# One transfer instead of two for the first tokens, and the first products over all four token tiles in turn

## The chip, the cores and the metric

The kernel runs on one core of a Trainium2 chip. Time is device time in microseconds (us) from launch to end; lower is better. The engines are PE (TensorE, matrix products; PEld are its loads of the stationary operand), DVE (VectorE), ACT (ScalarE), POOL (GpSimd) and SP, which here only issues transfers (DMAs).

## The reference

The input has 2048 tokens of 448 features. Two branches are computed from it and mixed by a gate per token. Branch A is attention with 16 heads of 28 features, in which every token sees itself and seven earlier ones at steps of two. Branch B is a dense layer to 1792 features, a squared ReLU, and a dense layer back.

```
qkv = x @ wqkv                      # 448 -> 3*448
a   = softmax(q . k[s-2w] * scale over w=0..7) @ v  @ wo
h   = relu(x @ w1 + b1)**2          # 448 -> 1792
b   = h @ w2 + b2
g   = sigmoid((x * gate_w).sum(-1))
out = g * a + (1 - g) * b
```

## The kernel before

All matrix operands are split into a high part, rounded to a shorter format, and a low part, the rest. A product of two numbers is then three products on PE: high x high, high x low, low x high. In the code the names end in `h` and `l` (`x.h`, `x.l`, `wqh`, `wql`).

The 448 features that are summed over lie in row tiles: three of 128 rows (k = 0, 1, 2) and a last one of 64. The tokens come in four chunks of 512, each of four token tiles of 128. One accumulator in PSUM holds the result of one token tile and one of q, k, v.

The kernel first computes q, k and v for all chunks, writes them to DRAM, and reads them back in the order that attention wants. Attention runs on POOL (products) and DVE (sums), beside the dense branch on PE. The order of instructions on each engine is the order of the code: a planner with an assumed PE clock (`advance`, `at`, `when`) decides at build time where the work of the other engines is put between the products.

The change lies at the very start. Before data is there, PE runs `WARM` products of zeros into a scratch accumulator (line 632). Meanwhile SP issues, for each row tile k, a transfer of the q weights (line 639) and one of the tokens of the first chunk (line 644); for k = 0 the tokens come in two transfers of 256 columns, token tiles 0 and 1 and then 2 and 3. Lines 654 to 665 split what arrives: ACT makes the high part of the weights (655) and of the tokens in two halves of columns (662), except for the first half of k = 0, which DVE makes (660); DVE makes the low parts (663 for the weights, 665 for the tokens, in halves).

`qkv_first` (line 257) then adds up q for the four token tiles of the first chunk. For each k it takes token tiles 0 and 1 through their three products, two by two, and then token tiles 2 and 3: twelve products of 128 rows and 450 columns per k, 36 in all (line 266). After them come the last row tile and the k and v products (line 188, through `side_by_side`), which use half of the array each and run in pairs.

Of the kernel before, what the change touches and what calls it, by code (L numbers as in the profile page):

```python
# [22 lines left out]
CH = 512  # L23
NQ = D + 2
# [23 lines left out]
LEAD = 5  # L48
DEFER = 2
ORDER = (3, 0, 1, 2)  # L50
WARM = 13
PP_BUFS = 4
ST_BUFS = 3
BT_BUFS = 8
# [3 lines left out]
def gated_mix_kernel(ctx: ExitStack, tc: tile.TileContext, xT, wqkv, w1, w2, wo, b1, b2, out):  # L58
    nc = tc.nc
# [72 lines left out]
    def x_tiles(c, pool):  # L132
        return X([pool.tile([P, 2, CH], F32R, tag=f"x{j}", name=f"x{c}_{j}") for j in range(4)])
# [34 lines left out]
    def block(b):  # L168

        o = (0, NP, NP + D)[b]  # L170
        return slice(o, o + ncols(b))
# [45 lines left out]
    def full(x, acc, tl, b, ks=range(3)):  # L217
        sl, n = slice(tl * P, tl * P + P), block(b)
        r = []
        for k in ks:  # L220
            r += [(acc, x.h[k][:, sl], wqh[:, k, n]), (acc, x.h[k][:, sl], wql[:, k, n]),
                  (acc, x.l[k][:, sl], wqh[:, k, n])]
        return r

    def last(x, acc, tl, b):

        sl = slice(tl * P, tl * P + P)
        n = block(1) if b == 2 else slice(0, ncols(b))
        h, l = w7h[:, n], w7l[:, n]
        return [(acc, x.x7[:, sl], h), (acc, x.x7[:, sl], l), (acc, x.x8[:, sl], h)]  # L230

    def accs(c, b, tls, tags):
        return [Acc(t, f"qkv{c}_{tl}_{b}", ncols(b)) for t, tl in zip(tags, tls)]

    def run(c, todo, steps):


        a = 0
        for e, done, *turns in steps:
            side_by_side(todo[0][a:e], todo[1][a:e])  # L240
            while a < e:
                n = min(12, e - a)
                if clock["on"] and a + n == e:

                    advance(max(n - LEAD, 0) * MM448)
                    while turns and not callable(turns[0]):
                        turn(*turns.pop(0))
                    n = min(n, LEAD)
                advance(n * MM448)
                a = min(a + 12, e)  # L250
            for t in turns:
                t() if callable(t) else turn(*t)
            for b, tl, acc in done:
                assert acc.todo == 0
                qkv_evacuate(acc.pt, c, tl, b)

    def qkv_first(x):


        four = range(4)  # L260
        q = accs(0, 0, four, "bbbb")
        for k in range(3):
            for two in ((0, 1), (2, 3)):
                for j, prods in enumerate(zip(*(full(x, q[i], i, 0, (k,)) for i in two))):
                    for acc, a, w in prods:
                        nc.tensor.matmul(acc.pt[:, :NQ], a, w, start=k == j == 0, stop=False)  # L266
            advance(12 * MM448)
        for acc in q:
            acc.todo = 3
        k = accs(0, 1, four, "mmmm")  # L270
        t = [sum((last(x, a[i], i, b) for i in four), []) for b, a in ((0, q), (1, k))]
        f = [full(x, k[i], i, 1) for i in four]
        run(0, [t[0] + f[0] + f[1] + f[2] + f[3], t[1] + f[2] + f[3] + f[0] + f[1]],
            [(3, [(0, 0, q[0])], (k[0], k[0])),
             (12, [(0, i, q[i]) for i in (1, 2, 3)], (k[1], k[1])),
             (24, [], (k[0], k[2])), (33, [], (k[1], k[3])),
             (39, [(1, 0, k[0]), (1, 2, k[2])]), (48, [(1, 1, k[1]), (1, 3, k[3])])])
        v = accs(0, 2, four, "bbbb")
        f, l = [full(x, v[i], i, 2) for i in four], [last(x, v[i], i, 2) for i in four]
        run(0, [f[0] + l[0] + f[2] + l[2] + f[1] + f[3], f[1] + l[1] + f[3] + l[3] + f[0] + f[2]],  # L280
            [(15, [], (v[0], v[1])), (24, [], (v[2], v[3])),
             (33, [(2, 0, v[0]), (2, 1, v[1])]), (42, [(2, 2, v[2]), (2, 3, v[3])])])
# [195 lines left out]
    def advance(dt):  # L478
        clock["pe"] += dt
        while due := [x for x in later if x[0] <= clock["pe"]]:  # L480
            item = min(due, key=lambda x: x[0])
            later.remove(item)
            item[1]()
        if not clock["on"]:
            clock["att"] = clock["pe"]
            return
        while clock["att"] < clock["pe"]:
            try:
                r = next(att)
            except StopIteration:  # L490
                clock["on"] = False
                return
            if r is None:
                clock["att"] = clock["pe"]
                return
            clock["att"] += r


    def raw_tile(name):
        return rawp.tile([P, 4, 512], F32, tag="raw", name=name)  # L500
# [129 lines left out]
    nc.vector.memset(none, 0.0)  # L630
    for _ in range(WARM):
        nc.tensor.matmul(warm[:, :2 * P], zero[:, :P], zero, start=True, stop=True)  # L632
# [3 lines left out]
    rx = raw_tile("xraw0")  # L636
    for k in range(4):
        if k < 3:
            nc.sync.dma_start(raws[0][:, k, :NQ], wqkv[0, :, k])
        else:  # L640
            for b, rows in ((0, slice(0, 64)), (1, slice(64, P))):
                nc.sync.dma_start(raws[0][rows, k, :NQ], wqkv[b, rows, k])
        for cols in ((slice(0, 256), slice(256, CH)) if k == 0 else (slice(0, CH),)):
            nc.sync.dma_start(rx[:, k, cols], xT[0, :, k, cols])

    for b, tag in ((1, "k"), (2, "v")):
        raw = attp.tile([P, 3, D], F32, tag=tag, name=f"wqraw{b}")
# [5 lines left out]
    x = x_tiles(0, xap)  # L653
# [93 lines left out]
    for c in range(4):  # L747
        x = xs[c]
        if c == 0:
            qkv_first(x)  # L750
        else:
            qkv_two(x, c, 0, copies=c == 3)
            qkv_two(x, c, 2, (mlp_one, mlp_two) if c == 3 else (), c == 3)
        if c == 1:
            st_["spilled"] = 0
            clock["on"] = True
            clock["att"] = clock["pe"] - 1.0
            advance(0.0)
        if c == 3:
            st_["spilled"] = 1  # L760
# [279 lines left out]
    c, x = ORDER[0], xm[3]  # L1040
# [8 lines left out]
    for g in range(2, 2 * NF):  # L1049
        i, f = g // (NF // 2), g % (NF // 2) * 2  # L1050
# [4 lines left out]
        if not f:  # L1055
            x, slots = X([nxt[j][0] for j in range(4)]), [nxt[j][1] for j in range(4)]
# [113 lines left out]
```

## Time and profile before

| | us |
|---|---|
| median of 3 runs | 415.18 |
| lowest, highest | 414.21, 415.46 |
| the profiled execution | 414.58 |
| its span, first to last instruction | 412.7 |
| PE busy | 408.4 (99%) |
| POOL, DVE, ACT busy | 268.6, 255.9, 211.9 |

The span leaves out 1.9 us of the execution's time that lie around it. In the profile a row of the timeline gives start, duration, engine, line, operation, what it writes and reads, and how many instructions are merged; in brackets stands the idle time before it and what ended that. Matrix products overlap at their ends, so the pace of a stream of them is read from their starts. "SPq" is the issue of a transfer, not the transfer itself.

### The profile page before, as it was taken

What the parts mean: (1) busy time and instruction counts of PE and PEld (TensorE: products, weight loads), DVE (VectorE), ACT (ScalarE), POOL (GpSimd) and SP (SyncE); (2) the same over time, 40 slices, a digit from 0 to 9 for tenths busy, and PEclk for the clock granted to TensorE, in tenths of its full rate; (3) what the DMA queues carried; (4) which work ended last, traced back from release to release, by engine and by line L of the source; (5) the groups of instructions that cost most, each with busy time, mean ns of one, the idle gap of its engine ahead of it and who ended that gap; (6) DMA issues with size and microseconds to landing.
All of it is one profiled execution on the core that took longest, in us unless ns stands there. A gap on an engine that the chain in (4) does not pass through costs nothing.

```text
span 412.7 us, 9323 instructions
## 1 busy us (share of the span) xinstructions
PE 408.4 (99%) x3835; PEld 377.6 (91%) x3835; DVE 255.9 (62%) x404; ACT 211.9 (51%) x477; POOL 268.6 (65%) x167
## 2 busy tenths in 40 slices
PE   8999999999999999999999999999999999999997
PEld 8999999999999999888888888989898888888996
DVE  4520523276767767777656798879576677892354
ACT  5642556378756565444565535444653254346540
POOL 0000000965989999999989899999899977860000
PEclk9999999999999999999999999999999999999999
DMA  7989799989164307654112649765145611168204
GB/s 236 380 318 326 227 364 292 363 259 321 47 224 159 128 2 258 207 186 152 37 50 93 233 157 266 200 149 149 24 163 192 224 46 59 72 175 139 91 0 180
DMA packets 65611, 73.76 MB, mean 179 GB/s; under 512 B 32352, under 2 KB 58528, under 8 KB 65184
## 3 DMA queue, kind: packets, MB, share of 16 engines
q1 hardware_dynamic: 65568, 73.16, 54.5%
q8 instruction: 30, 0.49, 0.5%
q14 instruction: 13, 0.11, 0.1%
HBM read 45.71 MB, written 28.25 MB: 179 GB/s over the span
## 4 chain that ended last, share of the span: by engine, by line
PE 99%; DVE 0%; issue 0%
PE b L188 33%; PE h L188 32%; PE qkv L188 23%; PE a L188 7%; PE qkv L266 2%; PE warm L632 1%; PE a L944 1%; PE last L944 0%; DVE bt L823 0%; PE last L936 0%; PE a L936 0%; DVE zero L629 0%; DVE b1z L630 0%
## 5 line engine op out<-in xcount | busy, mean ns | idle before, releaser
L339 POOL TENSOR_TENSOR qk<-q,k 128x896 f32<-128x896 f32 x64 | 135.0, 2138 | 83.2 <-DMA k<-k_d 78.9
L346 POOL TENSOR_TENSOR av<-lg,v 128x896 f32<-128x896 f32 x64 | 119.5, 1962 | 8.0 <-DVE lg L340 5.6
L188 PE MATMUL qkv<-wqh,x 64*128 64x448 f32 (+1 forms) x528 | 90.9, 360 | 0.0
L619 DVE TENSOR_TENSOR h<-h,h 128x512 fp32r<-128x512 f32 x56 | 38.3, 687 | 60.8 <-ACT h L622 60.4
L188 PEld LDWEIGHTS qkv<-wqh,x 64*128 64x128 f32 x528 | 74.0, 184 | 1.3
L188 PE MATMUL qkv<-wql,x 64*128 64x448 f32 (+1 forms) x264 | 74.7, 360 | 0.0
L188 PE MATMUL b<-w2ah,h 64*128 64x448 f32 x448 | 70.4, 359 | 0.0
L188 PE MATMUL b<-w2bh,h 64*128 64x448 f32 x448 | 69.6, 360 | 0.0
L340 DVE TENSOR_REDUCE lg<-qk 128x32 f32<-128x896 f32 x64 | 67.1, 1076 | 2.2 <-POOL qk L339 2.1
L354 DVE TENSOR_REDUCE o<-av 128x112 f32<-128x896 f32 x64 | 66.5, 1070 | 2.1 <-POOL av L346 1.8
L620 ACT ACTIVATE h<-h,b1z 128x512 f32<-128x512 f32 x56 | 36.7, 656 | 44.0 <-PE h L188 44.0
L188 PEld LDWEIGHTS b<-w2ah,h 64*128 64x128 f32 x448 | 48.0, 184 | 2.8
L188 PEld LDWEIGHTS b<-w2bh,h 64*128 64x128 f32 x448 | 46.0, 184 | 3.2 <-ACT h L571 0.3
L188 PE MATMUL b<-w2al,h 64*128 64x448 f32 x224 | 47.6, 358 | 0.0
L188 PEld LDWEIGHTS qkv<-wql,x 64*128 64x128 f32 x264 | 45.5, 184 | 0.7
L188 PE MATMUL b<-w2bl,h 64*128 64x448 f32 x224 | 45.8, 358 | 0.0
L207 ACT ACTIVATE st<-qkv 128x448 f32<-128x448 f32 x48 | 24.5, 543 | 32.2 <-PE qkv L188 27.1
L188 PE MATMUL h<-x,w1h 64*128 64x512 f32 x168 | 36.1, 386 | 0.0
L621 ACT ACTIVATE h<-h 128x512 fp32r<-128x512 f32 x56 | 33.5, 599 | 1.7
L622 ACT ACTIVATE h<-h 128x512 f32<-128x512 f32 x56 | 33.2, 593 | 0.0
L188 PE MATMUL h<-x,w1l 64*128 64x512 f32 x84 | 29.7, 386 | 0.0
L571 ACT ACTIVATE h<-h 128x4 fp32r<-128x4 f32 (+1 forms) x35 | 7.2, 206 | 42.6 <-PE b L188 42.4
(145 smaller groups left out, 749.4 us busy)
## 6 DMA issues: line engine op xcount, KB each, us to landing
k<-k_d SPq DMA_DIRECT2D x8, 840.0 KB, 6.7
v<-v_d SPq DMA_DIRECT2D x8, 840.0 KB, 4.4
x_d<-x SPq DMA_DIRECT2D x11, 512.0 KB, 6.0
q_d<-st SPq DMA_DIRECT2D x8, 448.0 KB, 4.6
k_d<-st SPq DMA_DIRECT2D x8, 448.0 KB, 4.1
v_d<-st SPq DMA_DIRECT2D x8, 448.0 KB, 7.1
w1raw<-w SPq DMA_DIRECT2D x4, 896.0 KB, 10.0
q<-q_d SPq DMA_DIRECT2D x8, 448.0 KB, 3.6
```

The costliest lines, as they stand in the source:

```text
L188: nc.tensor.matmul(acc.pt[:, :acc.n], a[rows], w[rows], start=acc.todo == acc.all, stop=acc.todo == 1)
L207: nc.scalar.activation(st[:, :, t % 2], pt[:, :D].rearrange("p (g c) -> p g c", g=G), AF.Copy)
L266: nc.tensor.matmul(acc.pt[:, :NQ], a, w, start=k == j == 0, stop=False)
L339: nc.gpsimd.tensor_mul(pr, q[:, s:s + 1].to_broadcast([P, W, C]), k[:, s:s + W])
L340: pending.append(lambda: nc.vector.tensor_reduce(lg[:, s], pr.rearrange("p w (h d) -> p w h d", h=HG), axis=AX.X, op=ALU.add))
L346: nc.gpsimd.tensor_mul(pr.rearrange("p (h d) w -> p w h d", h=HG), lg[:, s][:, :, :, None].to_broadcast([P, W, HG, DH]), v[:, s:s + W].rea ...
L354: nc.vector.tensor_reduce(o[:, g * C:(g + 1) * C], pr, axis=AX.X, op=ALU.add)
L571: nc.scalar.activation(ap, f32(ap), AF.Copy)
L619: nc.vector.tensor_sub(hl, pt, f32(hh))
L620: ops += [lambda pt=pt, r=r: nc.scalar.activation(pt, pt, AF.Relu, bias=b1t[:, f + r:f + r + 1]), lambda pt=pt, hh=hh: nc.scalar.activatio ...
L621: lambda pt=pt, hh=hh: nc.scalar.activation(hh, pt, AF.Square),
L622: lambda pt=pt, r=r, low=low: (nc.scalar.activation(pt, pt, AF.Square), at(delays[r], low))]
```

## The change

Three things change. The tokens of the first row tile are loaded by one transfer of 512 columns, as those of the other row tiles are. Within each row tile the three products go over all four token tiles in turn (high x high for tiles 0 to 3, then high x low, then low x high), instead of over two tiles and then the other two. And there are fourteen warm-up products instead of thirteen. The splitting on ACT and DVE keeps its halves and its order; no other instruction changes its place on any engine.

```diff
-WARM = 13
+WARM = 14
...
         for k in range(3):
-            for two in ((0, 1), (2, 3)):
-                for j, prods in enumerate(zip(*(full(x, q[i], i, 0, (k,)) for i in two))):
-                    for acc, a, w in prods:
-                        nc.tensor.matmul(acc.pt[:, :NQ], a, w, start=k == j == 0, stop=False)
+            for j, prods in enumerate(zip(*(full(x, q[i], i, 0, (k,)) for i in four))):
+                for acc, a, w in prods:
+                    nc.tensor.matmul(acc.pt[:, :NQ], a, w, start=k == j == 0, stop=False)
             advance(12 * MM448)
...
-        for cols in ((slice(0, 256), slice(256, CH)) if k == 0 else (slice(0, CH),)):
-            nc.sync.dma_start(rx[:, k, cols], xT[0, :, k, cols])
+        nc.sync.dma_start(rx[:, k], xT[0, :, k])
```

## The prediction

> **What bounds the kernel now.** I read the page's busy shares and chain first, then the chain of the first 20 us, since the diff touches nothing later, and then the timeline there. The page (sections 1 and 4):
>
> ```profile
> PE 408.4 (99%) x3835; PEld 377.6 (91%) x3835; DVE 255.9 (62%) x404; ACT 211.9 (51%) x477; POOL 268.6 (65%) x167
> PE 99%; DVE 0%; issue 0%
> ```
>
> The chain is PE from end to end, so a delay of the first real product reaches the end of the kernel unless a later PE wait takes it up. The waits of PE's products over the whole span have one entry, the wait ahead of the first warm-up product:
>
> ```profile
> PE warm L632 <- DVE b1z L630: 1.2, 1, 1.2
> ```
>
> So there is no later wait that could swallow a change, and none that could be removed. The chain of the first 20 us:
>
> ```profile
> 1.20 3.14 PE warm L632 x13
> 4.33 8.42 PE qkv L266 x36
> 12.76 7.28 PE qkv L188 x67
> ```
>
> All the change is in the first two rows. The timeline of PE alone there (start us, busy us), a narrow window for the last warm-up product first:
>
> ```profile
> 3.92 0.41 PE L632 MATMUL warm<-zero 128*128 128x256 f32 x1
> ...
> 4.13 1.03 PE L266 MATMUL qkv<-wqh,x 128*128 128x450 f32 x2
> 4.96 0.95 PE L266 MATMUL qkv<-wql,x 128*128 128x450 f32 x2
> 5.71 1.44 PE L266 MATMUL qkv<-wqh,x 128*128 128x450 f32 x4
> 6.99 0.57 PE L266 MATMUL qkv<-wql,x 128*128 128x450 f32 x2
> 7.39 0.96 PE L266 MATMUL qkv<-wqh,x 128*128 128x450 f32 x4
> 8.20 0.56 PE L266 MATMUL qkv<-wql,x 128*128 128x450 f32 x2
> ...
> 12.20 0.56 PE L266 MATMUL qkv<-wqh,x 128*128 128x450 f32 x2
> ```
>
> The starts give the pace; the busy times overlap. Two products from 4.96 to 5.71: 0.375 us each. Four from 7.39 to 8.20: 0.20 each. The four from 5.71 to 6.99 took 1.28 = 0.375 n + 0.20 (4 - n), so n = 2.7: the pace doubles at about 5.71 + 2.7 x 0.375 = 6.73. The two from 4.13 took 0.83 instead of 0.75, so the stream in effect starts at 4.21. From there the 36 products run without a stall: 6.7 slow (4.21 to 6.73), 29.3 x 0.20 = 5.86, end 12.59; the row at 12.20 plus two is 12.60.
>
> What the first products wait for, in the timeline of all engines:
>
> ```profile
> 0.75 0.39 SPq L639 DMA_DIRECT2D wqraw<-wqkv  x1
> 1.20 0.89 SPq L644 DMA_DIRECT2D xraw<-xT  x2
> 2.13 0.43 SPq L639 DMA_DIRECT2D wqraw<-wqkv  x1
> ...
> 3.34 0.58 ACT L655 ACTIVATE wqh<-wqraw 128x450 fp32r<-128x450 f32 x1 [1.31 <-DMA wqraw<-wqkv]
> 3.64 0.29 DVE L660 CAST x<-xraw 128x256 fp32r<-128x256 f32 x1 [2.50 <-DMA xraw<-xT]
> 3.95 0.63 DVE L663 TENSOR_TENSOR wql<-wqraw,wqh 128x450 fp32r<-128x450 f32 x1
> ...
> 4.05 0.50 PEld L266 LDWEIGHTS qkv<-wqh,x 128*128 128x128 f32 x2
> ...
> 4.49 0.42 DVE L665 TENSOR_TENSOR x<-xraw,x 128x256 fp32r<-128x256 f32 x1
> ...
> 5.54 0.42 ACT L662 ACTIVATE x<-xraw 128x256 fp32r<-128x256 f32 x1 [1.63 <-DMA xraw<-xT]
> ...
> 6.18 0.58 ACT L655 ACTIVATE wqh<-wqraw 128x450 fp32r<-128x450 f32 x1 [0.23 <-DMA wqraw<-wqkv]
> ...
> 6.93 0.72 ACT L662 ACTIVATE x<-xraw 128x256 fp32r<-128x256 f32 x2 [0.17 <-DMA xraw<-xT]
> ...
> 8.86 0.72 ACT L662 ACTIVATE x<-xraw 128x256 fp32r<-128x256 f32 x2 [0.73 <-DMA xraw<-xT]
> ```
>
> The first half of the tokens is cast at 3.64 to 3.93, the first weight load follows at 4.05, and the thirteenth warm-up product hands over at 4.13. Data and warm-up end together. The second half is there only at 5.54, for the products of tiles 2 and 3, which come at the seventh place, 6.46.
>
> **The change, part by part.** The profiled execution took 414.58 us for a span of 412.7; the median of the runs shown is 415.18.
>
> *One transfer of 512 columns.* It removes one issue of SP (0.89 for two, so about 0.45) and makes DVE's first cast, and with it the first product, wait for 256 KB instead of 128 KB. The DMA's share of time and its GB/s, the last two columns:
>
> ```profile
> 1.00:2.00 1.00, 0.80 (x3) 0.81 (x4) 0.14 (x2) 1.00 (x1) 0.39 (x8) 1.00 0.25 32
> 2.00:3.00 1.00, 1.00 (x6) 1.00 (x6) 0.00 (x0) 0.03 (x1) 0.00 (x0) 1.00 0.84 284
> 3.00:4.00 1.00, 1.00 (x7) 1.00 (x5) 0.34 (x2) 0.58 (x1) 0.00 (x0) 1.00 0.44 112
> 7.00:8.00 1.00, 1.00 (x7) 0.93 (x6) 1.00 (x3) 1.00 (x3) 0.00 (x0) 1.00 0.99 342
> ```
>
> The extra 131 kB at 342 GB/s take 0.38 us, at 284 GB/s 0.46. Bounds: nothing, if they fit into the idle 0.56 between 3.00 and 4.00 while the first half's completion is on its way anyway; 5.54 - 3.64 = 1.90, if the whole lands when its second half did. I take 0.38, since behind this transfer the queue was half empty and nothing competes. The cast then starts at about 4.02 and the stream at 4.21 + 0.38 = 4.59.
>
> *The fourteenth warm-up product.* The thirteenth starts at 3.92 and hands over at 4.13, so one takes 0.21. The fourteenth ends at 4.34, ahead of the data, so it costs nothing by itself; if the transfer cost nothing, it would be what is late, and the stream would start at 4.34, 0.13 later than now. That is the lower end.
>
> *What a later start costs.* A delay d falls into the slow stretch. If the pace doubles at 6.73 as before, d / 0.375 products move from the slow stretch to the fast one, where each takes 0.20: the end moves by 0.53 d. For 0.38 that is 0.20 us; for the bounds 0.13 and 1.90 it is 0.07 and 1.0.
>
> *Four tiles in turn.* The same 36 products, same shapes, same number of weight loads; only their order changes, and the schedule written out behind them is advanced by the same amount, so no later instruction moves on any engine. Each deadline: tile 2's high part is now wanted at the third place, 4.59 + 0.75 = 5.34. ACT, idle from 3.92 on, does that half beside DVE's cast, 4.02 to 4.44: in time. The low part of the weights is wanted fifth (6.1) and is done by about 4.02 + 0.29 + 0.02 + 0.63 = 4.96; the low part of the tokens ninth, done by 5.8 for both halves. So DVE gets more slack than now. In the second row tile all four token tiles' high parts are wanted within the first four products, which start at 6.73 + (12 - 5.7) x 0.20 = 7.99; ACT ends both halves at 6.93 + 0.72 = 7.65, and by one issue (0.45) sooner if SP's earlier issues reach the data. In the third, they start at 10.4, and ACT is through at 9.58. Nothing of this reaches the path. SP's queue moves up by one place from 1.65 on; the loads behind it (other weights, next tokens) wait for earlier transfers to land, and none has PE waiting now.
>
> **Sum:** 0.20 later, 0.05%. Onto 414.58 that is 414.8, onto the median 415.18 it is 415.4; I predict 415.1, between the two. The likeliest case's own range is 414.3 to 415.7: a cost from 0.07 to 0.53 x 0.46 = 0.24 on the lowest and the highest of the runs shown, 414.21 and 415.46. A difference below 0.3% (1.25 us, the spread of the three runs shown) can't be told from none.
>
> **Rivals.**
>
> 1. *The doubling of the pace comes later* (slower). Now PE runs from 1.20 with at most 0.08 us lost, and doubles at 6.73, 5.53 us in. With the transfer 0.38 later and one more warm-up product, PE would stand still for about 4.59 - 4.34 = 0.25 us. If a pause of that size sets the count back, the pace doubles 5.53 us after 4.59, at 10.12: 3.39 us more at the slow pace, of which 1 - 0.20/0.375 = 47% is lost, 1.58, plus 0.20: 416.4 on the profiled execution, 417.0 on the median. Against it: 0.08 us did no harm. It decides from a pause somewhere above 0.08, and needs the transfer later than 3.64 + 0.13. I give 0.17.
> The Trainium skill ("TensorE: Matmul & The Clock Gate", Part 1: The HAM clock gate) says the array runs at half rate until one window of about 3.4 us, which runs freely and does not start with the kernel, has been busy. The doubling from 0.375 to 0.20 agrees. By it a spoiled window would put the doubling one window on, about 10.1, with nearly the same price, and the place of the window would also move from run to run, which one execution can't show.
>
> 2. *The transfer lands late* (slower, but within the bound): packets of the next weights mix in and it lands as the second half did, at 5.54. The stream starts at 6.11, the end moves by 1.0: 415.6 to 416.2. For it: the half issued second took until 5.54 though it was issued by 2.09. Against: that half shared the queue with the next weights, of which the first half saw nothing. 0.10, with the pause of rival 1 then likely as well.
>
> 3. *The change costs nothing at the start and gains behind it* (slightly faster). In an execution in which the pace doubles early, at 5.0 say, the present order has tile 2 wait for ACT's second half (5.96 plus the 0.12 from the cast's end to the weight load: 6.08, where the stream would be at 5.76), and the second row tile for 7.47. The new order has no such wait and could start the second row tile at 5.0 + 11 x 0.20 = 7.2, if the transfer for it, issued 0.45 sooner, lands 0.27 sooner: a gain of 0.27, so 414.3 to 414.9. In the profiled execution that condition isn't met. 0.15.
>
> The forecast has the remaining 0.58.
>
> **How the numbers follow.** Rival 1 is slower by over 0.3% (0.4%), most of its 0.17; half of rival 2's chance, with its pause, as well (0.05); scatter of the runs about a small loss adds a little: slower 0.24. Faster by over 0.3% needs 1.25 us, which no mechanism here gives; the scatter of the runs, more under rival 3 than elsewhere, leaves 0.11. Same: 0.65. The range leaves out the upper part of rival 1 and the lowest scatter: 414.1 to 416.6.
>
> **What would show it.** Right: one transfer for the first tokens, DVE's first cast at 3.9 to 4.2 instead of 3.64, ACT's second half next to it, the first real product at about 4.5, pace 0.375 until about 6.7, the last of the 36 at about 12.6 instead of 12.40, and nothing else moved. Wrong: the cast later than 4.5; a doubling near 10; a PE wait inside the 36 products at a row tile's start; or a difference that arises behind 13 us, of which I have none.

## The result

The changed kernel takes 417.03 us (median of 8 runs, 415.41 to 417.47) against 414.33 (8 runs, 414.11 to 415.46): the ratio is 1.005, with a 95% interval from 1.0039 to 1.0061. By the ratio it is slower by about 2 us; the medians lie 2.7 apart, since the runs of the changed kernel fall into two groups, three from 415.4 to 416.3 and five from 416.9 to 417.5. The forecast was no measurable change, 415.1 in a range of 414.1 to 416.6. The profiled execution of the changed kernel took 416.26 us for a span of 414.5; it belongs to the shorter group.

The chain of the changed kernel's first 25 us (start us, us, what), which in the kernel before was PE throughout:

```profile
1.65 0.43 SPq L638
2.08 0.04 issue
2.12 6.41 DMA xraw<-xT
8.53 0.02 issue
8.55 0.42 ACT x L660
8.98 0.04 issue
9.02 5.09 PE qkv L265 x24
14.11 11.01 PE qkv L188 x104
```

A transfer of tokens stands in it now: the one of the second row tile, issued at 2.12. The first row tile's transfer is late as well, but in this execution the second one's lateness is what reached the end. The waits of PE have a new first entry (us in total, times, longest):

```profile
PE qkv L265 <- ACT x L660: 1.8, 2, 1.6
```

The timeline of PE of the same kernel, and from that of all engines the rows of what it waited for:

```profile
1.20 3.36 PE L631 MATMUL warm<-zero 128*128 128x256 f32 x14 [1.20 <-DVE b1z L629]
6.15 1.04 PE L265 MATMUL qkv<-wqh,x 128*128 128x450 f32 x4 [1.59 <-ACT x L660]
7.03 0.96 PE L265 MATMUL qkv<-wql,x 128*128 128x450 f32 x4
7.83 0.96 PE L265 MATMUL qkv<-wqh,x 128*128 128x450 f32 x4
9.02 1.09 PE L265 MATMUL qkv<-wqh,x 128*128 128x450 f32 x4 [0.24 <-ACT x L660]
...
14.04 0.47 PE L188 MATMUL qkv<-w7h,x 64*128 64x450 f32 x2
```

```profile
1.19 0.42 SPq L642 DMA_DIRECT2D xraw<-xT  x1
...
5.71 0.42 ACT L660 ACTIVATE x<-xraw 128x256 fp32r<-128x256 f32 x1 [1.64 <-DMA xraw<-xT]
5.71 0.29 DVE L658 CAST x<-xraw 128x256 fp32r<-128x256 f32 x1 [4.57 <-DMA xraw<-xT]
...
8.55 0.72 ACT L660 ACTIVATE x<-xraw 128x256 fp32r<-128x256 f32 x2 [1.45 <-DMA xraw<-xT]
```

The single transfer lands 4.5 us after its issue. The first cast starts at 5.71 instead of 3.64, and the first real product at 6.15 instead of 4.13. The next row tile's tokens are late too, 8.55 instead of 6.93, although their transfer was issued about 0.5 sooner, and PE waits a second time: four products from 7.83 would end at 8.63, the next starts at 9.02.

The account of the two profiled executions: the products of line 188 start at 14.04 instead of 12.69, 1.35 later. The first product is 2.02 later, the second wait costs 0.39, and the four products behind it take 0.93 instead of 0.80, another 0.13. Against that, the pace had already doubled in the standstill (0.22 per product from 6.15, 0.20 from 7.03), while the kernel before ran 6.7 products at 0.375, which saves 6.7 x 0.175 = 1.17. The sum is 1.37. Behind the start the distance stays at 1.36 up to 360 us. Then a wait for DVE stops PE's weight loads for 0.38, and the distance is 1.64 behind it and 1.74 at the last product:

```profile
363.94 0.18 PEld L188 LDWEIGHTS b<-w2bh,h 64*128 64x128 f32 x2 [0.38 <-DVE h L618]
```

The times differ by 1.68. This wait stands in some profiles of kernels with a late start (0.76 with 22 warm-up products, 0.51 with the later transfers held back) and not in others; what decides it stays open. The median lost 2.7, about 1 us more than this execution, and the experiments say why.

### The profile page after: what moved, and what is told of

It reads as the page before. It is cut to its first block, busy times and chain, and to the rows that moved or that the text cites. A ratio compares the mean times of both kernels' runs of the same rounds, so it can differ in the third digit from the quotient of the medians.

```text
span 414.5 us, 9323 instructions
## 1 busy us (share of the span) xinstructions
PE 408.3 (99%) x3836; PEld 376.7 (91%) x3836; DVE 255.8 (62%) x404; ACT 212.0 (51%) x477; POOL 268.6 (65%) x167
## 4 chain that ended last, share of the span: by engine, by line
PE 97%; DMA 2%; SPq 0%; DVE 0%; ACT 0%; issue 0%
PE b L188 33%; PE h L188 32%; PE qkv L188 23%; PE a L188 7%; DMA xraw<-xT 2%; PE qkv L265 1%; PE a L942 1%; PE last L942 0%; SPq L638 0%; DVE bt L821 0%; ACT x L660 0%; SPq L642 0%; PE last L934 0%; PE a L934 0%
```

## The experiments

Three theories stood against each other. D: the single transfer lands late, and this alone makes the loss. O: the new order of the products costs something by itself. G: the standstill of PE also puts off the doubling of its pace, at a price of its own.

**The transfer split again, all else as in the changed kernel.**

```diff
-        nc.sync.dma_start(rx[:, k], xT[0, :, k])
+        for cols in ((slice(0, 256), slice(256, CH)) if k == 0 else (slice(0, CH),)):
+            nc.sync.dma_start(rx[:, k, cols], xT[0, :, k, cols])
```

> The changed kernel with the first tokens loaded by two transfers again (four tiles in turn and 14 warm-up products stay). If the single transfer is the cause (theory D): the first real product is back at 4.1 to 4.4, and most of the 2.7 us between the medians goes. If the order of the products has a price of its own (theory O): token tile 2 is now wanted third, at about 4.35 + 0.75 = 5.1, and its high part is there only when ACT is through with the second half, at about 6.0, so PE stands still for about 1 us in front of the third product and the time lies 0.5 to 1 us above the kernel before (414.8 to 415.4), more if the pause also puts off the doubling of the pace.

Measured: 415.05 (12 runs), ratio to the kernel before 1.0016 (1.0002 to 1.0030). The runs lie between 414.64 and 416.89. Most of the loss is gone, as D says. PE in this kernel:

```profile
4.24 0.56 PE L265 MATMUL qkv<-wqh,x 128*128 128x450 f32 x2
5.86 0.68 PE L265 MATMUL qkv<-wqh,x 128*128 128x450 f32 x2 [1.06 <-ACT x L661]
```

The price of the order is there as well: the third product, token tile 2, waits 1.06 us for the second half. With the split transfer the order by twos is what hid that half's landing. In this execution the pace had doubled before the first product (0.56 for two at 4.24), so the wait cost little at the end (line 188 starts at 12.87 instead of 12.69); in the longer ones the pause may also have put off the doubling, which these runs don't show.

**The single transfer alone, in the kernel before.**

```diff
-        for cols in ((slice(0, 256), slice(256, CH)) if k == 0 else (slice(0, CH),)):
-            nc.sync.dma_start(rx[:, k, cols], xT[0, :, k, cols])
+        nc.sync.dma_start(rx[:, k], xT[0, :, k])
```

> The kernel before with one change, the single transfer (two tiles at a time and 13 warm-up products stay). Theory D: the first real product at about 6.1, as in the changed kernel, and the whole loss: 416.5 to 417.5. If the order or the fourteenth warm-up product had a part in the loss, it stays clearly below that, at 415 to 416.

Measured: 417.34 (5 runs), ratio 1.0057 (1.0036 to 1.0077): the whole loss, with neither the new order nor the fourteenth warm-up product. Its profiled execution took 417.34 too, and shows the missing microsecond:

```profile
1.20 3.14 PE L632 MATMUL warm<-zero 128*128 128x256 f32 x13 [1.20 <-DVE b1z L630]
5.93 1.09 PE L266 MATMUL qkv<-wqh,x 128*128 128x450 f32 x2 [1.59 <-ACT x L661]
6.82 0.95 PE L266 MATMUL qkv<-wql,x 128*128 128x450 f32 x2
7.57 1.70 PE L266 MATMUL qkv<-wqh,x 128*128 128x450 f32 x4
9.07 0.95 PE L266 MATMUL qkv<-wql,x 128*128 128x450 f32 x2
9.82 1.28 PE L266 MATMUL qkv<-wqh,x 128*128 128x450 f32 x4
10.94 0.56 PE L266 MATMUL qkv<-wql,x 128*128 128x450 f32 x2
```

Here the pace is still 0.375 from 7.57 to 9.82, and the four products from 9.82 to 10.94 put the doubling at about 10.5. The ten products ahead of 9.82 and 1.8 of those four are slow, 11.8 instead of 6.7: 5.1 x 0.175 = 0.89 us more. With the start 1.80 later and 0.06 more for the first two products (0.89 against 0.83) that is 2.75, and the time is 2.76 above the 414.58 of the kernel before's profiled execution. In the changed kernel's profile the doubling happened to fall into the standstill.

**Fourteen warm-up products alone, in the kernel before.**

```diff
-WARM = 13
+WARM = 14
```

> The kernel before with a fourteenth warm-up product alone. The first real product starts 0.2 us later, and the end moves by 0.1 us: 414.6 to 414.9, no difference that can be told.

Measured: 414.56 (10 runs), ratio 1.0002 (0.9993 to 1.0012). Nothing, as expected.

**The standstill filled: 22 warm-up products in the changed kernel.**

```diff
-WARM = 14
+WARM = 22
```

> The changed kernel with 22 instead of 14 warm-up products, so that PE is busy until about 6.06 when all are slow, just ahead of the first real product at 6.15. Theory G (the standstill of 1.8 us puts off the doubling of the pace in many executions): the doubling comes while the warm-up still runs or shortly behind, and the median falls from 417.0 to 415.5 to 416.0. Without G: 417.0 as before, since no real product starts sooner.

Measured: 416.08 (11 runs), ratio 1.0026 (1.0012 to 1.0040). The changed kernel had 1.0050. Nothing real starts sooner by more than 0.24:

```profile
1.19 4.88 PE L631 MATMUL warm<-zero 128*128 128x256 f32 x22 [1.19 <-DVE b1z L629]
5.91 0.98 PE L265 MATMUL qkv<-wqh,x 128*128 128x450 f32 x4
6.74 0.99 PE L265 MATMUL qkv<-wql,x 128*128 128x450 f32 x4
```

Its tokens came sooner than in the changed kernel's profile, at 5.17 instead of 5.71, but PE was busy with the warm-up until 6.08:

```profile
5.17 0.29 DVE L658 CAST x<-xraw 128x256 fp32r<-128x256 f32 x1 [4.03 <-DMA xraw<-xT]
```

Products of zeros win back about 1 us. That is what G says; the second row tile's tokens, at 7.87 instead of 8.55 in this execution, may have a part in it, which the next experiment does without.

**The standstill alone: 5 warm-up products in the kernel before, with its data in time.**

```diff
-WARM = 13
+WARM = 5
```

> The kernel before with 5 instead of 13 warm-up products: all data as before, but PE stands still for about 1.8 us from 2.3 to 4.1. Theory G measured by itself: the doubling of the pace moves by up to 3.4 us, and the median rises by 0.5 to 1.6 us (414.9 to 415.9), with a wider spread. Without G: 414.3, no change.

Measured: 415.81 (11 runs), ratio 1.0032 (1.0018 to 1.0046), the runs from 414.75 to 417.04. G measured by itself: a standstill of 1.5 us in front of a product that is on time costs 1.2 us by the medians (415.81 against 414.65) and 1.3 by the ratio, about what filling it gains. G holds. The profiled execution is the shortest of them, and even there the pace stays slow longer, four products from 5.78 to 7.28 at 0.375 each instead of a doubling at 6.73:

```profile
4.14 1.09 PE L266 MATMUL qkv<-wqh,x 128*128 128x450 f32 x2 [1.51 <-DVE x L660]
5.03 0.95 PE L266 MATMUL qkv<-wql,x 128*128 128x450 f32 x2
5.78 1.69 PE L266 MATMUL qkv<-wqh,x 128*128 128x450 f32 x4
7.28 0.60 PE L266 MATMUL qkv<-wql,x 128*128 128x450 f32 x2
```

This leaves the question of the prediction's main term: why does a transfer of 256 KB land at 5.7 and not at 4.0?

**Tokens ahead of weights.** The changed kernel with the two first transfers in the other order.

```diff
     for k in range(4):
+        if k == 0:
+            nc.sync.dma_start(rx[:, k], xT[0, :, k])
...
-        nc.sync.dma_start(rx[:, k], xT[0, :, k])
+        if k:
+            nc.sync.dma_start(rx[:, k], xT[0, :, k])
```

> The changed kernel with the first tokens' transfer issued ahead of the first weights' instead of behind it. If the lateness belongs to what comes second (the transfers slow down from about 3.3 us on, whatever is under way): the tokens land at about 3.5, the weights at 5.0 to 5.7, and the first real product is no earlier, at about 6.1. If reading the tokens is slow by itself (their place in memory, their 2048-byte rows): the tokens again land at 5.0 or later.

Measured: 417.11 (one run). From the timeline:

```profile
4.77 0.29 DVE L661 CAST x<-xraw 128x256 fp32r<-128x256 f32 x1 [3.62 <-DMA xraw<-xT]
...
5.44 0.58 ACT L656 ACTIVATE wqh<-wqraw 128x450 fp32r<-128x450 f32 x1 [3.42 <-DMA wqraw<-wqkv]
```

First in the queue, the tokens still take 4.0 us from their issue at 0.75; the weights in that place took 2.6. They are neither as early as the first guess had it (3.5) nor as late as the second (5.0), but slow in this place too. The weights, now second and issued at 1.20, are late as well, and it is they that the chain shows:

```profile
1.20 4.22 DMA wqraw<-wqkv
```

So this run doesn't decide between the two guesses: the tokens are slow in the first place, and what stands behind them is late with them.

**All loads held back.**

```diff
     rx = raw_tile("xraw0")
+    nc.gpsimd.memset(raws[0][:, 0, :NQ], 0.0)
+    nc.gpsimd.memset(raws[0][:, 0, :NQ], 0.0)
```

> The changed kernel with all loads held back by two fills of the first weight tile on POOL, about 1 us. If the slow stretch lies at a fixed time (3.3 to 5.2 us): the weights themselves now fall into it and land late, and the tokens soon after 5.7. If it goes with the order or the amount of what is moved: it moves along by about 1 us, the weights land at about 4.4 and the tokens at about 6.6.

Measured: 419.50 (one run). The first loads are issued at 2.36 and 2.81:

```profile
5.12 0.58 ACT L655 ACTIVATE wqh<-wqraw 128x450 fp32r<-128x450 f32 x1 [3.11 <-DMA wqraw<-wqkv]
```

```profile
7.55 1.84 PE L265 MATMUL qkv<-wqh,x 128*128 128x450 f32 x4 [3.02 <-ACT x L662]
```

The weights take 2.76, as in the changed kernel, and the first product follows 4.74 after the tokens' issue (4.96 in the changed kernel). The slow stretch moves along with the transfers; it is not at a fixed time. The hold was 1.6 us, more than the 1 us meant.

**Later transfers held back,** so that the first two are alone.

```diff
         if k < 3:
+            if k == 1:
+                for _ in range(5):
+                    nc.gpsimd.memset(raws[0][:, 1, :NQ], 0.0)
             nc.sync.dma_start(raws[0][:, k, :NQ], wqkv[0, :, k])
```

> The changed kernel with the transfers behind the first two held back by five fills of the second weight tile on POOL, to an issue at about 3.5 to 4 instead of 1.65. If later transfers mixing in make the first tokens late (rival 2 of the prediction): they now land at 3.7 to 4.0, the first real product comes at about 4.5, while the second row tile comes later, so the time lies anywhere from 415 to 417. If the slow stretch doesn't come from the later transfers: the tokens land at 5.1 to 5.7 all the same and the time is 417 or more.

Measured: 416.51 (10 runs), ratio 1.0043 (1.0028 to 1.0059).

```profile
3.96 0.33 SPq L641 DMA_DIRECT2D wqraw<-wqkv  x1
4.33 0.43 SPq L645 DMA_DIRECT2D xraw<-xT  x1
4.75 0.29 DVE L661 CAST x<-xraw 128x256 fp32r<-128x256 f32 x1 [3.62 <-DMA xraw<-xT]
```

The tokens are there at 4.75, between the two guesses. Against the 5.71 of the changed kernel the followers account for about 1 us, but the landing varies: with the same followers the first cast came at 5.17 with 22 warm-up products and at 5.49 with the single transfer in the kernel before, so 0.4 to 1 us. Another 0.7 us against the expected 4.02 is left to the transfer alone.

**The tokens laid out differently in DRAM.** The 128 rows of 2048 bytes that the first transfer reads lie 8192 bytes apart, since each partition holds its four row tiles one after the other. In one kernel the first chunk lies row tile by row tile, so the rows are next to each other; in the other each partition's four rows are padded by 512 bytes together, so that the step is 8704 bytes, for all four chunks.

```diff
+    x0 = xT[0].rearrange("p k n -> (p k n)").rearrange("(k p n) -> p k n", k=4, p=P)
...
-        nc.sync.dma_start(rx[:, k], xT[0, :, k])
+        nc.sync.dma_start(rx[:, k], x0[:, k])
...
-        "xT": _np.stack([ktiles(xp[c]) for c in range(4)]),
+        "xT": _np.stack([ktiles(xp[0]).transpose(1, 0, 2).reshape(P, 4, CH)] + [ktiles(xp[c]) for c in range(1, 4)]),
```

> The changed kernel with the first chunk of tokens laid out in DRAM one row tile after the other, so that the 128 rows of 2 KB of the first transfer lie next to each other instead of 8192 bytes apart. If the wide steps through DRAM make the tokens late: they land at 3.7 to 4.1, the first real product comes at 4.3 to 4.6, and the time falls to 414.5 to 415.3. If not: landing at 5.1 to 5.7 and 417 as in the changed kernel.

```diff
-        nc.sync.dma_start(raw[:, :, :CH], xT[c])
+        nc.sync.dma_start(raw[:, :, :CH], xT[c, :, :4 * CH].rearrange("p (k n) -> p k n", k=4))
...
-        nc.sync.dma_start(rx[:, k], xT[0, :, k])
+        nc.sync.dma_start(rx[:, k], xT[0, :, k * CH:k * CH + CH])
...
-        "xT": _np.stack([ktiles(xp[c]) for c in range(4)]),
+        "xT": _np.pad(_np.stack([ktiles(xp[c]) for c in range(4)]).reshape(4, P, 4 * CH), ((0, 0), (0, 0), (0, 128))),
```

> The changed kernel with the token rows in DRAM 8704 bytes apart (512 bytes of padding) instead of 8192. If it is the power of two that makes the step slow, the first tokens land at 3.7 to 4.2 here too; if rows must lie close together, they land at 5.0 or later as in the changed kernel.

Measured: next to each other 414.70 (10 runs), ratio to the kernel before 1.0006 (0.9995 to 1.0016); padded 414.74 (one run). The first cast of the one and of the other:

```profile
4.00 0.30 DVE L659 CAST x<-xraw 128x256 fp32r<-128x256 f32 x1 [2.86 <-DMA xraw<-xT]
```

```profile
4.00 0.30 DVE L658 CAST x<-xraw 128x256 fp32r<-128x256 f32 x1 [2.86 <-DMA xraw<-xT]
```

Both start at 4.00, with the followers in the queue as in the changed kernel. What the DMA moved between 3 and 5 us (last two columns: share of time, GB/s), in the changed kernel and with padding:

```profile
3.00:4.00 1.00, 1.00 (x7) 1.00 (x6) 0.00 (x0) 0.51 (x1) 0.00 (x0) 1.00 0.74 123
4.00:5.00 1.00, 0.55 (x3) 0.26 (x2) 0.00 (x0) 0.07 (x1) 0.00 (x0) 1.00 0.60 107
```

```profile
3.00:4.00 1.00, 1.00 (x7) 1.00 (x6) 0.00 (x1) 0.58 (x2) 0.00 (x0) 1.00 0.88 285
4.00:5.00 1.00, 1.00 (x5) 0.80 (x5) 1.00 (x3) 0.42 (x1) 0.00 (x0) 1.00 0.92 258
```

More than twice the rate from 512 bytes of padding, with the same sizes, order and followers. The step of 8192 bytes between the rows is the cause of the late landing, and followers hurt only together with it. The weights, 128 rows of 1800 bytes at a step of 7200, were no slower in any of these kernels when they were first (2.6 to 2.8 us from issue to use).

**The kernel before with its tokens next to each other** (the first layout above, on the kernel before).

> The kernel before (two transfers, two tiles at a time, 13 warm-up products) with the first chunk's tokens next to each other in DRAM. The second half of the tokens lands well before 5.4 if the wide steps are slow; but no product waited for it, and the first one starts where the warm-up ends, so the time stays within 0.5 us of the kernel before whichever theory holds.

Measured: 414.59 (11 runs), ratio 0.9998 (0.9990 to 1.0007). The second half is split at 4.92 instead of 5.54, and nobody waited for it:

```profile
4.92 0.42 ACT L663 ACTIVATE x<-xraw 128x256 fp32r<-128x256 f32 x1 [0.86 <-DMA xraw<-xT]
```

The first half, at the same step of 8192 bytes in the kernel before, was not late there: cast at 3.64, and at 3.80 here. So the step by itself doesn't slow every transfer; it showed in what came behind the first 128 KB.

No version beat the kernel before.

## Why the prediction was wrong

- **The transfer** is the step that failed: "I take 0.38, since behind this transfer the queue was half empty and nothing competes." The cast came 2.07 later (3.64 to 5.71), and 1.53 to 1.85 later in the two other profiles with the same first loads (5.17 and 5.49), where the upper bound was 1.90. The half-empty queue between 3 and 4 us was not room: the second half of the same rows was under way in it. With the rows next to each other the same stretch of the kernel before shows a share of 0.80 and 170 GB/s instead of 0.44 and 112:

```profile
3.00:4.00 1.00, 1.00 (x7) 1.00 (x5) 0.20 (x1) 0.52 (x1) 0.00 (x0) 1.00 0.80 170
```

The clue stood in the quoted rows: the second half, issued by 2.09, landed at 5.54. I gave it to the weights mixing in. Where the rows don't lie 8192 bytes apart, the term is right, in one profile of each layout: 0.36 for a cast at 4.00, and a median of 414.70 where 414.8 to 415.4 had been worked out.
- **What a later start costs** failed with it: "If the pace doubles at 6.73 as before". With the single transfer alone it doubled at about 10.5, which cost 0.89 more.
- **Rival 2** (late landing, 0.10) named the place and a landing within 0.2 us, but priced it with the doubling at 6.73: 1.0. Its mechanism, the next weights' packets, is a part only: alone, the transfer still needs until 4.75, and with padding those packets do no harm.
- **Rival 1** (the doubling put off, 0.17) is real: 1.2 to 1.3 us measured by itself, where 1.58 had been worked out for a whole set-back. That its 417.0 is the measured median is luck: it was made of a start 0.38 late and a pause of 0.25, and the runs showed a start about 2 late and a pause of 1.6. The prediction called the pause "then likely as well" under rival 2, but gave the two together no price; it is about 1.8 + 1.0 = 2.8, since a late transfer makes the standstill.
The Trainium skill's rule quoted there ("TensorE: Matmul & The Clock Gate", Part 1: The HAM clock gate), a window that runs freely, fits the scatter of the doubling in the profiles: ahead of the first product at 6.15 in the changed kernel, at 6.73 in the kernel before, at about 7.3 with five warm-up products, at about 10.5 with the single transfer alone. No run here shows the length of the window.
- **Rival 3** (a gain where the pace doubles early, 0.15): the wait it names does occur, in the profile of the kernel before with fourteen warm-up products, where the pace doubled early and the seventh product started at 6.00, behind the ACT cast from 5.53. The changed kernel could gain nothing from it, since its own tokens came later still; with the rows next to each other it was no faster in the median either.
- **The order of the products** was priced at nothing on the ground that the second half arrives with the first. In the changed kernel that is so; with the transfer split it costs 1.06 us of waiting. For the second row tile, "ACT ends both halves at 6.93 + 0.72 = 7.65, and by one issue (0.45) sooner if SP's earlier issues reach the data" failed with the transfers: the tokens came at 8.55, and PE waited until 9.02.
- **The fourteenth warm-up product** costs nothing: right.
- "a difference that arises behind 13 us, of which I have none": in the profiled execution 0.38 of the 1.74 arose from 363 us on.

## What to carry to other kernels

A queue that is half idle while transfers are under way is no room to be filled: ask first what holds the transfer that is in it. Where rows are read at a step of 8192 bytes (other powers of two beyond 2048 were not tried), try a padded row before cutting the transfer or ordering the work around its lateness. And a late first operand on PE is to be priced together with what the standstill does to its pace, since the cause brings both.

## What the runs showed of the hardware

A transfer of 128 rows of 2 KB into 128 partitions took 4.0 to 4.5 us from issue to use with the rows 8192 bytes apart and other transfers behind it, 3.6 without those, and 2.8 with the rows at steps of 8704 or 2048 bytes; the rate between 4 and 5 us was 107 against 258 GB/s. Why was not shown, nor why the first transfer of half those rows, 1 KB each, was not slow (2.4). The Trainium skill ("DMA: Bandwidth & Descriptors", Latency and other measured facts) lists rates that fall with row pitches of large powers of two, from 207 GB/s at 512 KiB to 103 at 4 MiB, and says that 4 KiB of padding restored the full rate at 4 MiB and 192 bytes did not. The runs here agree in kind at a pitch of 8 KiB, far below those, where 512 bytes of padding were enough.

PE standing still for 1.5 to 1.6 us in its first 6 us cost about 1 us beyond the wait (1.0050 to 1.0026 when filled, 1.0000 to 1.0032 when made), and products of zeros were enough to prevent it. The granted clock in the profile's windows reads 1.00 throughout, also where products run at 0.375 instead of 0.20: the pace of the starts shows it, that column does not.
